# Mixed k/q tail tile first, in the single banks; z and kv of the first two head pairs ahead of later projections

## The chip, the cores and the metric

The kernel runs on one core of one Trainium2 chip. The metric is device time in microseconds (us) of one execution. Times of a kernel are the median of several runs; the profile is of one further execution. The engines are PE (TensorE, matmul), DVE (VectorE), ACT (ScalarE), POOL (GpSimd) and SP (SyncE, which here issues most DMAs).

## What is computed

A feature-map attention, and on its output a two-layer feed-forward network with a leaky activation. Batch 8, 8 heads, 576 tokens, head width 64, 128 features:

```python
def phi(x):
    proj = np.einsum('bhsd,df->bhsf', x, w_phi)
    proj = proj - np.max(np.abs(proj), axis=-1, keepdims=True)
    return np.concatenate([np.exp(proj), np.exp(-proj)], axis=-1)
q_p, k_p = (phi(q), phi(k))
kv = np.einsum('bhsf,bhsd->bhfd', k_p, v)
z = np.sum(k_p, axis=2)
num = np.einsum('bhsf,bhfd->bhsd', q_p, kv)
den = np.einsum('bhsf,bhf->bhs', q_p, z)[..., None] + 1e-06
x = num / den                      # then reshaped to 4608 tokens x 512
h = x @ w_in
g = np.maximum(h, 0.0) + alpha * np.minimum(h, 0.0)
out = g @ w_out                    # w_in 512 x 2048, w_out 2048 x 512
```

All is float32. The feed-forward matmuls split every operand into a high and a low part and add three products.

## The kernel before

Attention works on 32 **pairs** of heads; the two heads of a pair are h = 0 and 1. A pair's k and q are loaded as one tile `raw` of 1152 columns: 512 of k, then 64 of k's tail and 64 of q's tail, then 512 of q. `project` multiplies them by `w_phi` in nine tiles of 128 columns per head: chunk 0 is k's first four tiles; chunk 1 is the **mixed tile** (both tails) and q's four tiles. A projection lies in PSUM until DVE has taken the maximum of its absolute values (L324) and written the difference to an SBUF tile `t` (L325). Then ACT takes the exponentials: `xk` from chunk 0 (L338) and `k` from the mixed tile (L333). PE sums k's features (`k_z`, L378: z) and multiplies them with v (`k_acc`, L361: kv). ACT copies the result (`ks`), PE transposes it (`kt`), ACT copies that (`sf`). PE also transposes the q part of `t` (`qt`: `q_turn(2)` is the mixed tile, `q_turn(0)` and `q_turn(1)` the four q tiles of each head), ACT takes its exponentials (`qf`), and PE forms the denominator (`d`, L444) and the numerator (`n`, L426).

Where the projections lie in PSUM: a pair of banks for one chunk of both heads, tile `pj` (pool `ps_pj`, one buffer, so the next chunk waits until DVE has read it); chunk 0 of the first two pairs lies in the two single banks of `psf` instead. Chunk 1 has ten tiles, two more than fit, and the fifth of each head lies in a single bank of `ps_m`, tile `pl`. `ps_m` has three buffers that `pl`, `kt`, the mixed `qt`, `d` and `n` take in turn. Before, `pl` holds the last q tile (j = 4), and the mixed tile (j = 0) lies in `pj` with three q tiles. `ps_kv` has one buffer for z and kv.

The two PE passes that a float32 matmul takes here are counted apart in the trace (x16 for eight matmuls).

What sets the order: every step of every pair is a function with a due time, i + an entry of `places(i)`; decoding of the 64-bit weights (`aw`, `ew`: L177 on ACT, L185 to L188 on DVE, L193 on POOL, L128 the cast, L132 the low part) and the feed-forward steps have due times as well. All are sorted, and the instructions of PE, SP, DVE and ACT stand in that order; each engine works through its list in order:

```python
with tc.manual_schedule(engines=pinned):
    for _, u in sorted(todo, key=lambda tu: tu[0]):
        u()
```

For the first nine pairs (`i < ZP`) z is summed by PE over all five k tiles. The feed-forward network's first part runs among the later pairs, its second part after them.

Of the kernel before, what the change touches and what calls it, by code (L numbers as in the profile page):

```python
# [38 lines left out]
WA = (0.0040, 0.50)  # L39
# [19 lines left out]
def places(i):  # L59
    early = i < ZP  # L60
    end = i >= NPAIR - 2
    return dict(
        ld=-1.90,
        lv=-0.80,
        p=(-0.9955 if early else -0.993, 0.0),
        ke=(-0.26, 0.0011),
        ks=(0.0015, 0.0022, 0.0026),
        kz=1.0002,
        ka=1.0012,
        ko=1.0025,  # L70
        kr=1.10,
        kc=1.16,
        q=(1.34, 1.50, 1.20),
        qe=(1.46, 1.62, 1.28),
        d=2.0004,
        ds=2.0008,
        n=2.005,
        s=2.0055,
        d9=2.25,
        dv=3.0016 if early else 3.20 if end else 2.80,  # L80
        rd=3.0017 if early else 3.21 if end else 2.82,
        rr=3.20 if early else 3.45 if end else 3.001,
        x=3.45 if early else 3.60 if end else 3.20,
        xs=3.90 if early else 3.85 if end else 3.45,
    )


F0 = 9.23
# [25 lines left out]
def fused_kernel(ctx: ExitStack, tc: tile.TileContext, kq, v, w_phi, w_in, w_out, alpha, out):  # L114
# [110 lines left out]
    def decode_at(t, blk):  # L225
        return [(t + (WT if t < TL else WL)[k], lambda u=u: u(*blk, WN)) for k, u in stages.items()]
# [58 lines left out]
    def attention_units(i):  # L285
# [12 lines left out]
        def project(ch):  # L298
            t = c["t", ch] = wk.tile([P, 2, 4 + ch, FD], F32, tag=f"t{ch}", name=f"t{i}_{ch}", bufs=1 + ch)
            dst, out, js = {}, [], [0, 1, 2, 3]  # L300
            if ch:
                js = [4] + js
                for h in range(2):
                    p1 = ps_m.tile([P, 1, 1, FD], F32, tag="m", name=f"pl{i}_{h}")
                    dst[h, 4] = p1[:, 0, 0]
                    out.append((slice(h, h + 1), slice(4, 5), p1))
            if ch == 0 and i < 2:
                for h in range(2):
                    p1 = psf.tile([P, 1, 4, FD], F32, tag="f", name=f"pj{i}_{ch}_{h}")
                    dst.update({(h, j): p1[:, 0, j] for j in range(4)})  # L310
                    out.append((slice(h, h + 1), slice(0, 4), p1))
            else:
                p2 = ps_pj.tile([P, 2, 4, FD], F32, tag="pj", name=f"pj{i}_{ch}")
                dst.update({(h, j): p2[:, h, j] for h in range(2) for j in range(4)})
                out.append((slice(0, 2), slice(0, 4), p2))
            for j in js:
                for h in range(2):
                    hs = slice(h * D, (h + 1) * D)
                    ts = slice((4 * ch + j) * P, (4 * ch + j + 1) * P)
                    pe.matmul(dst[h, j], lhsT=c["raw"][hs, ts], rhs=w_sb[hs], start=True, stop=True)  # L320
            for n, (hs, js, src) in enumerate(out):
                nh, nj = hs.stop - hs.start, js.stop - js.start
                m = wk.tile([P, nh, nj], F32, tag="m", name=f"m{i}_{ch}_{n}", bufs=4)
                dve.tensor_reduce(m, src, axis=AX.X, op=ALU.max, apply_absolute_value=True)  # L324
                dve.tensor_tensor(  # L325
                    t[:, hs, js], src, m.unsqueeze(3).broadcast_to([P, nh, nj, FD]), op=ALU.subtract
                )
# [150 lines left out]
        def store():  # L478
            nc.sync.dma_start(x_d[hp, :, b * S : (b + 1) * S], c["s"])

        at = places(i)
        us = [
            (at["ld"], load),
# [17 lines left out]
        for n in range(2):  # L501
            us.append((at["p"][n], lambda n=n: project(n)))
# [128 lines left out]
    todo = []  # L631
# [6 lines left out]
    first = [(ff, z, o) for z in range(2) for ff in range(NF1) for o in range(0, 512, WN)]  # L638
# [1 line left out]
    late += [(ff, z) for z in (1, 0) for ff in range(NF1 + NA, NF - NL)]  # L640
    blocks = [(ff, z, o) for ff, z in late for o in range(0, 512, WN)]
    for n, blk in enumerate(first):
        todo += decode_at(1 + n // 2 + WA[n % 2], blk)
    for n, blk in enumerate(blocks):
        todo += decode_at(W2A + W2D * n, blk)
    todo += first_x()
# [188 lines left out]
```

## Time and profile before

| | us |
|---|---|
| median of 3 runs | 1132.63 |
| lowest, highest of them | 1130.05, 1133.77 |
| the profiled execution | 1131.19 |
| its span in the profile | 1129.4 |
| PE busy in that span | 1115.0 |
| DVE, ACT, POOL busy | 643.2, 560.4, 211.0 |

The profiled execution's own time is 1.8 us above its span. The mean granted clock of PE is 0.997 of full speed over the span. Busy times overlap, since the engines work side by side; where PE is busy nearly all the time, what counts is when it is idle or at a lower clock, and what it waited for.

### The profile page before, as it was taken

The numbers are of one execution on the slowest core, as the hardware profiler recorded it, in microseconds if no ns is written. First come the engines' busy times: TensorE is split into PE (matmuls) and PEld (weight loads), VectorE is DVE, ScalarE is ACT, GpSimd is POOL, SyncE is SP. The second block draws the span as 40 slices with busy tenths as digits, with TensorE's granted clock in tenths as the row PEclk, the third lists the DMA queues.
The fourth block names the chain that finished last, engine by engine and source line by source line (L and its number), as shares of the span: only waits on it lengthen the run. The fifth ranks groups of instructions, "written<-read, shape, count | busy, mean of one in ns | idle before, by whom it ended". The sixth has DMA issues, their size and how long they took to land.

```text
span 1129.4 us, 18395 instructions
## 1 busy us (share of the span) xinstructions
PE 1115.0 (99%) x7246; PEld 868.8 (77%) x7246; DVE 643.2 (57%) x983; ACT 560.4 (50%) x1148; POOL 211.0 (19%) x217
## 2 busy tenths in 40 slices
PE   8999999999999999999999999999999999999998
PEld 6766777777777777677778888888888888888886
DVE  7888958798788787836862332424233423343323
ACT  4777665666666665665543342333333333333331
POOL 1244332322324242243541000000000000000000
PEclk8999999999999999999999999999999999999999
DMA  5566265546546365467627030303030302020011
GB/s 191 146 184 208 86 202 154 172 151 192 176 148 199 109 204 164 147 212 218 223 66 256 27 109 1 112 1 112 1 112 1 112 1 97 16 91 21 11 64 38
DMA packets 74389, 133.68 MB, mean 118 GB/s; under 512 B 14656, under 2 KB 25024, under 8 KB 73664
## 3 DMA queue, kind: packets, MB, share of 16 engines
q1 hardware_dynamic: 72000, 122.48, 33.9%
q0 software_dynamic: 2016, 9.96, 2.6%
q8 instruction: 57, 0.93, 0.3%
q14 instruction: 28, 0.23, 0.1%
q10 hardware_dynamic: 288, 0.07, 0.0%
HBM read 93.92 MB, written 38.42 MB: 117 GB/s over the span
## 4 chain that ended last, share of the span: by engine, by line
PE 93%; DVE 4%; ACT 1%; DMA 1%; issue 1%; POOL 0%; DVEq 0%; ACTq 0%
PE h L516 12%; PE h L518 11%; PE h L517 11%; PE po L523 8%; PE po L525 8%; PE po L527 8%; PE kv L361 6%; PE pj L320 5%; PE n L426 5%; PE o L523 4%; PE o L527 3%; PE o L525 3%; PE d L444 2%; PE qt L407 2%; PE kv L378 2%; PE pl L320 1%
## 5 line engine op out<-in xcount | busy, mean ns | idle before, releaser
L247 DVE SCALAR_TENSOR_TENSOR g<-r,aln,g 128x512 f32<-128x512 f32 x144 | 112.2, 779 | 309.2 <-ACT g L243 308.9
L242 ACT ACTIVATE r<-h 128x512 f32<-128x512 f32 x143 | 86.0, 601 | 279.1 <-PE h L518 279.0
L132 DVE TENSOR_TENSOR gl<-g,gh 128x512 fp32r<-128x512 f32 x144 | 105.1, 730 | 81.3 <-ACT gh L128 80.8
L128 ACT CAST gh<-g 128x512 fp32r<-128x512 f32 x144 | 90.0, 625 | 94.4 <-DVE g L247 94.4
L243 ACT ACTIVATE g<-h 128x512 f32<-128x512 f32 x144 | 86.0, 597 | 7.1 <-DVE r L240 6.4
L523 PE MATMUL po<-gh,wd 128*128 128x512 f32 x216 | 84.3, 390 | 0.2 <-ACT gh L128 0.2
L525 PE MATMUL po<-gh,wd 128*128 128x512 f32 x216 | 84.3, 390 | 0.0
L527 PE MATMUL po<-gl,wd 128*128 128x512 f32 x216 | 83.9, 390 | 0.0
L324 DVE TENSOR_REDUCE m<-pj 128x8 f32<-128x1024 f32 (+1 forms) x66 | 78.1, 1184 | 9.2 <-PE pj L320 9.1
L193 POOL TENSOR_TENSOR aw<-ew,aw 128x256 f32<-128x256 f32 x64 | 55.9, 874 | 131.8 <-DVE ew L188 130.3
L325 DVE TENSOR_TENSOR t<-pj,m 128x1024 f32<-128x1024 f32 (+1 forms) x66 | 78.7, 1192 | 2.3
L320 PEld LDWEIGHTS pj<-w_sb,raw 64*128 64x128 f32 x1024 | 63.4, 190 | 18.6 <-issue 13.8
L320 PE MATMUL pj<-w_sb,raw 64*128 64x128 f32 x1024 | 72.8, 281 | 4.7 <-DVE t L325 4.5
L523 PE MATMUL o<-gh,w 128*128 128x512 f32 x180 | 76.0, 422 | 0.2
L516 PE MATMUL h<-xh,w 128*128 128x512 f32 x180 | 75.8, 421 | 0.0
L527 PE MATMUL o<-gl,w 128*128 128x512 f32 x180 | 71.2, 396 | 3.1 <-DVE gl L132 2.9
L476 POOL TENSOR_TENSOR s<-s,rr 128x576 f32<-128x576 f32 x32 | 47.6, 1486 | 142.0 <-DMA rr<-rec_d 131.4
L417 ACT ACTIVATE qf<-qt 128x512 f32<-128x512 f32 x128 | 68.5, 615 | 6.3 <-PE qt L407 6.3
L518 PE MATMUL h<-xl,w 128*128 128x512 f32 x180 | 70.7, 393 | 0.0
L525 PE MATMUL o<-gh,w 128*128 128x512 f32 x180 | 70.6, 392 | 0.0
L517 PE MATMUL h<-xh,w 128*128 128x512 f32 x180 | 70.5, 392 | 0.0
L523 PE MATMUL po<-gh,w 128*128 128x512 f32 x180 | 70.1, 389 | 0.0
(110 smaller groups left out, 2415.5 us busy)
## 6 DMA issues: line engine op xcount, KB each, us to landing
xr<-x_d SPq DMA_DIRECT2D x18, 1024.0 KB
raw<-kq_dram SPq DMA_DIRECT2D x31, 576.0 KB
v<-v_dram SPq DMA_DIRECT2D x32, 320.0 KB
w_d<-raww SPq DMA_DIRECT2D x38, 256.0 KB
rr<-rec_d SPq DMA_DIRECT2D x64, 144.0 KB
x_d<-s SPq DMA_DIRECT2D x32, 288.0 KB
part_d<-os SPq DMA_DIRECT2D x36, 256.0 KB
pt<-part_d SPq DMA_DIRECT2D x9, 1024.0 KB
```

The source lines that it names most:

```text
L128: return act.copy(dst, src)
L132: return eng.tensor_tensor(dst, src, f(hi), op=ALU.subtract)
L242: act.activation(st["r"], ps, AF.Relu, scale=-1.0)
L243: act.activation(st["g"], ps, AF.Relu)
L247: dve.scalar_tensor_tensor(g, st["r"], aln[:, ff : ff + 1], g, op0=ALU.mult, op1=ALU.add)
L320: pe.matmul(dst[h, j], lhsT=c["raw"][hs, ts], rhs=w_sb[hs], start=True, stop=True)
L516: pe.matmul(ps, lhsT=wt[0][:, ws], rhs=xh, start=n == 0, stop=False)
L517: pe.matmul(ps, lhsT=wt[1][:, ws], rhs=xh, start=False, stop=False)
L518: pe.matmul(ps, lhsT=wt[0][:, ws], rhs=xl, start=False, stop=n == NK - 1)
L523: pe.matmul(ps, lhsT=wt[2][:, ws], rhs=gh, start=first, stop=False)
L525: pe.matmul(ps, lhsT=wt[3][:, ws], rhs=gh, start=False, stop=False)
L527: pe.matmul(ps, lhsT=wt[2][:, ws], rhs=gl, start=False, stop=last)
```

## The change

It has three parts. In chunk 1 the mixed tile goes to the single banks `pl` and is multiplied first, and q's four tiles go to the pair of banks `pj`. For pairs 0 and 1 other due times are put in place of those of `places`: z, kv and the copy of the first pair come before the projection of pair 1's chunk 1 (0.737), pair 1's z before chunk 0 of pair 2 and its kv right behind it, and the steps of pair 0 behind them move (`kr` to `n`). The decode of the first weight block is due 0.024 earlier.

```diff
@@ places
     early = i < ZP
     end = i >= NPAIR - 2
+    first = {}
+    if i == 0:
+        first = dict(
+            kz=0.7370, ka=0.7372, ko=0.7374, kr=1.0030, kc=1.0034,
+            n=2.0041, q=(1.0032, 1.0033, 1.0031), qe=(1.0036, 1.0037, 1.0035),
+        )
+    if i == 1:
+        first = dict(kz=0.0044, ka=0.0046, ko=0.0048)
     return dict(
...
-    )
+    ) | first
@@ project
             if ch:
-                js = [4] + js
+                js = js + [4]
                 for h in range(2):
                     p1 = ps_m.tile([P, 1, 1, FD], F32, tag="m", name=f"pl{i}_{h}")
-                    dst[h, 4] = p1[:, 0, 0]
-                    out.append((slice(h, h + 1), slice(4, 5), p1))
+                    dst[h, 0] = p1[:, 0, 0]
+                    out.append((slice(h, h + 1), slice(0, 1), p1))
...
                 p2 = ps_pj.tile([P, 2, 4, FD], F32, tag="pj", name=f"pj{i}_{ch}")
-                dst.update({(h, j): p2[:, h, j] for h in range(2) for j in range(4)})
-                out.append((slice(0, 2), slice(0, 4), p2))
+                dst.update({(h, ch + j): p2[:, h, j] for h in range(2) for j in range(4)})
+                out.append((slice(0, 2), slice(ch, ch + 4), p2))
@@ the list of steps
     for n, blk in enumerate(first):
-        todo += decode_at(1 + n // 2 + WA[n % 2], blk)
+        todo += decode_at(1 + n // 2 + (WA[n % 2] if n else -0.02), blk)
```

The instructions stay the same in number and shape, and the orders of SP and POOL do not change. PE's, DVE's and ACT's lists differ only up to the first transposes of pair 1 (`kt` of pair 1). Three places follow. In the names, `pj_0`, `pl_0` and so on carry the chunk or head, and the last number is the tile's; line numbers are 8 higher in the changed kernel.

PE, from the end of pair 1's chunk 0 (`raw_157` is pair 1's, `raw_206` pair 2's; `kv_242` and `kv_214` are pair 0's z and kv), before:

```order
L320 MATMUL pj_0_1_191<-w_sb,raw_157 128x128
L320 MATMUL pl_0_220<-w_sb,raw_157 128x128
L320 MATMUL pl_1_221<-w_sb,raw_157 128x128
L320 MATMUL pj_1_222<-w_sb,raw_157 128x128 x8
L378 MATMUL kv_242<-xk_161,ones 32x128 x16
L378 MATMUL kv_242<-k_0_130,ones 32x128 x4
L361 MATMUL kv_242<-xk_161,v_159 64x256 x8
L361 MATMUL kv_242<-k_0_130,v_159 64x256 x2
L320 MATMUL pj_0_283<-w_sb,raw_206 128x128 x8
L393 MATMUL kt_295<-ident,ks_275 128x128 x3
```

The same place of the changed kernel:

```order
L328 MATMUL pj_0_1_191<-w_sb,raw_157 128x128
L386 MATMUL kv_214<-xk_161,ones 32x128 x16
L386 MATMUL kv_214<-k_0_130,ones 32x128 x4
L369 MATMUL kv_214<-xk_161,v_159 64x256 x8
L369 MATMUL kv_214<-k_0_130,v_159 64x256 x2
L328 MATMUL pl_0_258<-w_sb,raw_157 128x128
L328 MATMUL pl_1_259<-w_sb,raw_157 128x128
L328 MATMUL pj_1_260<-w_sb,raw_157 128x128 x8
L401 MATMUL kt_282<-ident,ks_245 128x128 x3
L412 MATMUL qt_2_286<-ident,t_1_164 128x128 x2
```

Pair 0's z and kv now stand ahead of pair 1's chunk 1, and pair 2's chunk 0 has gone from between kv and `kt`.

DVE, from the last subtraction of pair 1's chunk 0 (`aw_0_0`, `ew_0_0` are the first weight block), before:

```order
L325 TENSOR_TENSOR t_0_189<-pj_0_1_191,m_0_1_203 128x512
L324 TENSOR_REDUCE m_1_0_233<-pl_0_220 128x1
L325 TENSOR_TENSOR t_1_219<-pl_0_220,m_1_0_233 128x128
L324 TENSOR_REDUCE m_1_1_236<-pl_1_221 128x1
L325 TENSOR_TENSOR t_1_219<-pl_1_221,m_1_1_236 128x128
L324 TENSOR_REDUCE m_1_2_239<-pj_1_222 128x8
L325 TENSOR_TENSOR t_1_219<-pj_1_222,m_1_2_239 128x2x512
L185 TENSOR_SCALAR aw_0_0_215<-aw_0_0_215 128x256
L186 SCALAR_TENSOR_TENSOR aw_0_0_215<-raww_0_0_210,aw_0_0_215 128x256
L187 TENSOR_SCALAR ew_0_0_277<-aw_0_0_215 128x256
L188 SCALAR_TENSOR_TENSOR ew_0_0_277<-raww_0_0_210,ew_0_0_277 128x256
L324 TENSOR_REDUCE m_0_0_292<-pj_0_283 128x8
```

The same place of the changed kernel:

```order
L333 TENSOR_TENSOR t_0_189<-pj_0_1_191,m_0_1_203 128x512
L193 TENSOR_SCALAR aw_0_0_212<-aw_0_0_212 128x256
L194 SCALAR_TENSOR_TENSOR aw_0_0_212<-raww_0_0_210,aw_0_0_212 128x256
L195 TENSOR_SCALAR ew_0_0_252<-aw_0_0_212 128x256
L196 SCALAR_TENSOR_TENSOR ew_0_0_252<-raww_0_0_210,ew_0_0_252 128x256
L332 TENSOR_REDUCE m_1_0_271<-pl_0_258 128x1
L333 TENSOR_TENSOR t_1_257<-pl_0_258,m_1_0_271 128x128
L332 TENSOR_REDUCE m_1_1_274<-pl_1_259 128x1
L333 TENSOR_TENSOR t_1_257<-pl_1_259,m_1_1_274 128x128
L332 TENSOR_REDUCE m_1_2_277<-pj_1_260 128x8
L333 TENSOR_TENSOR t_1_257<-pj_1_260,m_1_2_277 128x2x512
L332 TENSOR_REDUCE m_0_0_339<-pj_0_330 128x8
```

The four decode instructions have moved from behind pair 1's chunk 1 to ahead of it, so that pair 1's chunk 1 and pair 2's chunk 0 stand next to each other.

PE, from pair 1's z to the numerator of pair 0, in the changed kernel (`kv_308` is pair 1's, `raw_354` pair 3's; before, the order was z of pair 1, `d`, kv of pair 1, chunk 0 of pair 3, `n`, with pair 2's chunk 1 ahead of all):

```order
L386 MATMUL kv_308<-xk_247,ones 32x128 x16
L386 MATMUL kv_308<-k_1_132,ones 32x128 x4
L328 MATMUL pj_0_330<-w_sb,raw_206 128x128 x8
L369 MATMUL kv_308<-xk_247,v_208 64x256 x8
L369 MATMUL kv_308<-k_1_132,v_208 64x256 x2
L328 MATMUL pl_0_381<-w_sb,raw_206 128x128
L328 MATMUL pl_1_382<-w_sb,raw_206 128x128
L328 MATMUL pj_1_383<-w_sb,raw_206 128x128 x8
L452 MATMUL d_403<-qf_301,sf_299 32x288 x8
L434 MATMUL n_0_421<-qf_301,sf_299 64x288 x4
L434 MATMUL n_1_426<-qf_301,sf_299 64x288 x4
L328 MATMUL pj_0_432<-w_sb,raw_354 128x128 x8
```

Pair 2's chunk 1 now stands behind pair 1's kv, and the numerator of pair 0 stands ahead of pair 3's chunk 0.

## Rows read from the trace of the kernel before

**Rows 1.** The page, part 1: busy time, share, instructions by engine.

```profile
PE 1115.0 (99%) x7246; PEld 868.8 (77%) x7246; DVE 643.2 (57%) x983; ACT 560.4 (50%) x1148; POOL 211.0 (19%) x217
```

**Rows 2.** Timeline of PE: start, us, instructions, [idle before <- releaser].

```profile
8.25 1.01 PE L320 MATMUL pj<-w_sb,raw 64*128 64x128 f32 x13 [0.36 <-DVE t L325]
...
11.69 2.08 PE L320 MATMUL pj<-w_sb,raw 64*128 64x128 f32 x16 [2.09 <-DVE t L325]
...
22.81 1.16 PE L320 MATMUL pj<-w_sb,raw 64*128 64x128 f32 x16 [0.59 <-DVE t L325]
...
29.50 2.16 PE L426 MATMUL n<-qf,sf 128*64 128x288 f32 x16
31.60 0.55 PE L393 MATMUL kt<-ident,ks 128*128 128x128 f32 x3
...
33.49 1.06 PE L320 MATMUL pj<-w_sb,raw 64*128 64x128 f32 x16
...
98.93 1.16 PE L320 MATMUL pj<-w_sb,raw 64*128 64x128 f32 x16 [1.05 <-DVE t L325]
...
394.95 1.16 PE L320 MATMUL pj<-w_sb,raw 64*128 64x128 f32 x16 [0.37 <-DVE t L325]
...
467.27 0.50 PE L527 MATMUL o<-gl,w 128*128 128x512 f32 x1 [1.56 <-DVE gl L132]
```

**Rows 3.** Windows: length, busy time (x) PE PEld DVE ACT POOL, PEclk, DMA, GB/s.

```profile
10.50:11.00 0.50, 0.00 (x0) 0.00 (x0) 0.50 (x1) 0.00 (x0) 0.00 (x0) 0.76 0.92 354
...
13.50:14.00 0.50, 0.50 (x12) 0.28 (x12) 0.47 (x2) 0.00 (x0) 0.00 (x0) 0.50 0.05 20
...
17.50:18.00 0.50, 0.50 (x8) 0.32 (x6) 0.47 (x3) 0.27 (x1) 0.00 (x0) 0.92 0.72 230
...
466.00:467.00 1.00, 0.00 (x0) 0.00 (x0) 1.00 (x2) 0.00 (x0) 0.00 (x0) 1.00 0.48 49
```

**Rows 4.** Chain that ended last, 0 to 40 us: start, us, what.

```profile
13.77 2.29 PE kv L378 x40
16.06 3.07 PE kv L361 x20
...
23.97 1.23 PE kv L378 x40
...
26.17 2.31 PE kv L361 x20
```

**Rows 5.** Timeline of DVE, 8 to 34 us.

```profile
10.32 1.22 DVE L325 TENSOR_TENSOR t<-pj,m 128x1024 f32<-128x1024 f32 x1
...
13.58 0.69 DVE L325 TENSOR_TENSOR t<-pj,m 128x512 f32<-128x512 f32 x1
14.18 0.28 DVE L324 TENSOR_REDUCE m<-pl 128x1 f32<-128x128 f32 x1
...
15.23 1.21 DVE L324 TENSOR_REDUCE m<-pj 128x8 f32<-128x1024 f32 x1
...
17.62 0.28 DVE L185 TENSOR_SCALAR aw<-aw 128x256 uint32<-128x256 uint32 x1
...
18.72 0.43 DVE L188 SCALAR_TENSOR_TENSOR ew<-raww,ew 128x256 f32<-128x256 uint32 x1
20.28 1.22 DVE L324 TENSOR_REDUCE m<-pj 128x8 f32<-128x1024 f32 x1 [1.13 <-PE pj L320]
21.54 1.22 DVE L325 TENSOR_TENSOR t<-pj,m 128x1024 f32<-128x1024 f32 x1
...
30.88 1.22 DVE L325 TENSOR_TENSOR t<-pj,m 128x1024 f32<-128x1024 f32 x1
```

**Rows 6.** Timeline of ACT, 7 to 20 us.

```profile
8.14 2.00 ACT L338 ACTIVATE xk<-t 128x1024 f32<-128x1024 f32 x2 [5.19 <-DVE t L325]
11.58 0.72 ACT L333 ACTIVATE k<-t 64x256 f32<-64x256 f32 x2 [1.44 <-DVE t L325]
...
19.19 0.48 ACT L388 COPY ks<-kv 128x384 f32<-128x384 f32 x1 [0.73 <-PE kv L361]
```

**Rows 7.** Waits, 100 to 450 us: us in total, times, longest us.

```profile
ACT k L333 <- DVE t L325: 39.0, 21, 3.8
```

## The prediction

> **What bounds the kernel now.** I read the page's busy times first. PE is busy for 1115.0 of 1129.4 us [rows 1], so a change can save only what PE idles (14.4 us in all) or loses at a lower clock. The second view is PE's timeline with the idle time ahead of each entry [rows 2]. Of the longer idle stretches two lie where the change moves work: 2.09 us ahead of pair 1's chunk 1 at 11.69, and 0.59 us ahead of pair 2's chunk 1 at 22.81. Both end with DVE's subtraction, because the pair of banks has one buffer. Between 22.81 and 95 us PE does not wait at all. The later waits are 1.05 us at 98.93, 0.37 at 394.95 and 1.56 at 467.27, the last in feed-forward work.
>
> The third view is the granted clock. It falls during the 2.09 us: the window from 10.5 to 11.0 has a mean of 0.76, so with levels 1 and 0.5 the fall lies at 10.76; the window from 17.5 to 18.0 has 0.92, so the return lies at 17.58 [rows 3]. For 6.8 us PE ran at 1.2 instead of 2.4 GHz. What that cost is read from like work in both states: the projection took 2.08 us against 1.16 [rows 2], z 2.29 against 1.23, kv 3.07 against 2.31 [rows 4]. Together 0.92 + 1.06 + 0.76 = 2.74 us.
>
> So PE lost 2.09 + 0.59 + 2.74 = 5.4 us here, 0.48% of the time. That is the whole prize of the start. The fourth view, DVE's timeline, says how much of it is out of reach [rows 5]: from 10.32 to 32.10 (30.88 + 1.22, the end of pair 3's chunk 0) DVE has hardly any idle time but 1.13 us. DVE is nearly as much the limit of these 22 us as PE.
>
> **The change, part by part.** *Mixed tile in the single banks.* Number and shape of matmuls and DVE operations stay. DVE takes the single banks first, so the mixed tile's `t` is there one pair-of-banks operation earlier, and ACT's `k` need not wait for it. In pair 0 ACT ends `xk` at 8.14 + 2.00 = 10.14, waits 1.44 us and ends `k` at 12.30 [rows 6]; now `k` ends at 10.14 + 0.72 = 10.86. In the later pairs ACT's waits for `t`, 39.0 us over 21 waits [rows 7], mostly go. ACT is not what PE waits for there: the only wait for attention inside that stretch that rows 2 show is 0.37 us, on DVE. I cost the steady part at 0, with bounds of 0 and a gain of 0.37 + 1.05. The four q tiles now all come from the pair of banks, which was the last to be read before too, so the transposes of q are no later.
>
> *z and kv of pair 0 ahead.* PE ends pair 1's chunk 0 at about 9.3 (8.25 + 1.01 [rows 2]) and then waits for `xk` until 10.2: 0.9 us idle in place of 2.09. At full clock z ends at 10.2 + 1.23 = 11.4 (`k` is there at 10.86) and kv at 11.4 + 2.31 = 13.7 [rows 4]. Pair 1's chunk 1 then finds its banks free, since DVE has left them at 11.54 (10.32 + 1.22): `pl` takes 0.3 (4 of 16 parts of a 1.16), `pj` 1.16, to 15.2. `kt` follows to 15.7.
>
> *The decode ahead of pair 1's chunk 1 on DVE.* DVE ends pair 1's chunk 0 at 13.58 + 0.69 = 14.27 and now runs the four decode instructions, 18.72 + 0.43 - 17.62 = 1.53 us [rows 5], to 15.8. Their data must have landed: the queue moves 20 GB/s from 13.5 to 14.0 [rows 3], so the burst is over by then. Queued behind them on DVE is `pl` of pair 1, 15.23 - 14.18 = 1.05 us for both heads. The mixed `qt` of pair 0 waits for the buffer of the first `pl`, free at 15.8 + 0.52 = 16.3: **PE idles 0.6 us**. The transposes end at about 17.5 and z of pair 1 at 18.7. (`kt` and transposes take 33.49 - 31.60 - 0.3 = 1.6 us [rows 2].)
>
> *Pair 2's chunk 0 behind pair 1's z.* DVE ends pair 1's chunk 1 at 16.85 + 2.48 = 19.3 (2.48 is 21.54 + 1.22 - 20.28 [rows 5]). The banks free then: **PE idles 0.65**, projects from 19.35 to 20.5, and **DVE idles 1.2** meanwhile, since the decode that used to stand in this place is gone from it. Before, the like idle was 1.13 in spite of the decode, because of PE's half clock; so the gain of the clock is lost to the order here. DVE ends pair 2's chunk 0 at 23.0. PE does kv of pair 1 (to 22.8), `pl` (23.1), `pj` of pair 2 (24.2) and `d` (25.2; its length is 26.17 - 23.97 - 1.23 = 0.97 [rows 4]).
>
> *The second decode block.* Its scale on ACT stands behind `ks` of pair 1, which waits for kv at 22.8; `ks` takes 0.48 [rows 6], the scale about as much, so DVE **idles 0.75** to 23.75, decodes to 25.3, and takes 0.15 for `aln`. The first half of n needs the buffer of pair 2's first `pl`, free at 25.45 + 0.52 = 26.0: **PE idles 0.8**. n takes 31.60 - 29.50 = 2.1 [rows 2], to 28.1. DVE ends `pl` at 26.5 and pair 2's chunk 1 at 29.0, so pair 3's chunk 0 starts at 29.0: **PE idles 0.9**. It ends at 30.15; `kt`, transposes and `pl` bring PE to 32.05. DVE decodes to 30.5 and ends pair 3's chunk 0 at 33.0: **PE idles 1.0** and starts pair 3's chunk 1 at 33.05.
>
> *Sum.* The same step started at 33.49 before [rows 2]. From here both lists are the same and PE is the limit, so the gain is 33.49 - 33.05 = **0.45 us**: 1131.19 - 0.45 = 1130.7 for a run like the profiled one. That run lies 1.44 below the median shown, so in terms of the median I say 1132.63 - 0.45 = **1132.2 us**. Of the 5.4 us lost before, 0.9 + 0.6 + 0.65 + 0.8 + 0.9 + 1.0 = 4.85 come back as idle stretches of PE.
>
> *The clock.* The sum holds the clock at full speed. In the trace the 2.09 us stretch went with a fall, and the 1.56 us one at 467.27 did not: in the window from 466 to 467 PE is idle throughout and the clock stays at 1.00 [rows 2, 3]. Each new stretch is 1.0 or shorter, so by the rows I expect no fall, though there are six within 23 us. The Trainium skill, TensorE: Matmul & The Clock Gate, section "A second HAM failure mode: psum-queue depth-cycling", says that short idles between groups of matmuls, as PSUM banks are cycled, can make the clock swing between its levels. By the rows the sum stays a gain of 0.45; by that rule the rivals with falls below come in. No run here shows yet which holds for gaps of this length.
>
> **The rivals.**
>
> *One fall of the clock, as before.* If the first idle stretch still tips the clock at 10.76, and it returns at 17.58, then z, kv and pair 1's projection pay up to 2.74 us. DVE's decode hides part: `pj` of pair 1 would end at 17.9 instead of 15.2, where DVE comes to it at 16.85, so some 1.1 is lost there and more at the small steps behind: 1.1 to 2.7, say 1.9. Time 1132.2 + 1.9 = 1134.1, slower by 0.13%, which a measurement of this kernel can hardly tell from no change (0.3%, 3.4 us).
>
> *Faster: DVE gives way.* If the changed order kept DVE busy, without any of the 1.13 us idle, it would end pair 3's chunk 0 at 30.97, and PE could start the next step at 31.0: a gain of 2.5. With the later DVE waits gone too (1.05 + 0.37, since ACT runs ahead) it is 3.9: 1128.7 us. Against it: the two DVE idle stretches above follow from one buffer for the pair of banks, and the change adds none.
>
> *Slower: a swinging clock.* The six stretches lie close together between 9 and 33 us. One mechanism turns the sign: PE at 1.2 GHz for a second spell like that of before. Each spell costs up to 2.74 us in 6.8 us. The first, partly hidden, costs 1.9; a second, at 25 to 32 us, falls on d, n and projections with PE waited for by DVE, and costs 2.74: 1132.2 + 1.9 + 2.74 = 1136.8 us. It is slower by over 0.3% from 3.4 + 0.45 = 3.85 us of unhidden loss on, about nine and a half us at half clock.
>
> **How the numbers follow.** The forecast (no fall, gain 0.45) has 0.58; one fall 0.22; the faster case 0.10; the swinging clock 0.10. The first two are within 0.3%, hence faster 0.10, same 0.80, slower 0.10. The predicted time is 1132.2. The range has to take in the spread of the runs of before, 1130.05 to 1133.77, the bound of the waits (a gain of 2.5 alone gives 1130.1, with the later ones 1128.7) and one fall with its whole price (1132.2 + 2.7 = 1134.9): 1128.8 to 1135.2, which leaves out the far end of the faster case and the swinging clock.
>
> **What the profile after would show.** Right: z of pair 0 starts near 10.2; the 2.09 us stretch is gone; PE has idle stretches of 0.5 to 1 us ahead of the mixed `qt` of pair 0, pair 2's chunk 0, n of pair 0, pair 3's chunk 0 and pair 3's chunk 1, all ended by DVE; DVE idles about 1.2 us ahead of pair 2's chunk 0 and 0.75 ahead of the second decode; pair 3's chunk 1 starts near 33; ACT's waits of `k` for `t` shrink from 39 us to a few, with PE's time unmoved by that. Wrong: a window of half clock between 10 and 35 us (a rival with falls); pair 3's chunk 1 starting before 32 (DVE was not the limit); PE's idle stretches past 90 us gone or grown by over 1 us (ACT's lead counts after all); or PE busy time itself changed by over 3 us, which no step here provides for.

## The result, and the profile after

The changed kernel takes 1133.74 us as median of 20 runs (1131.75 to 1136.20), the kernel before 1131.28 beside it (20 runs, 1129.56 to 1133.77): a ratio of 1.0020, 95% interval 1.0013 to 1.0027. It is slower by about 2.3 us, where 0.45 us of gain were forecast. That is within the range and within 0.3%, but on the other side, and the interval excludes no change. (A ratio compares all executions of two kernels; it need not be the quotient of the two medians.)

The page of the changed kernel, its span and part 1 (compare [rows 1]):

```profile
span 1134.3 us, 18397 instructions
...
PE 1117.1 (98%) x7246; PEld 868.7 (77%) x7246; DVE 639.2 (56%) x983; ACT 561.9 (50%) x1148; POOL 213.0 (19%) x217
```

This profiled execution took 1136.04 us, near the top of its runs. PE is busy 2.1 us longer than before and idle 17.2 instead of 14.4 us. The timeline of PE (start, us, instructions, idle before it and what ended that), answering to [rows 2]:

```profile
8.97 1.13 PE L328 MATMUL pj<-w_sb,raw 64*128 64x128 f32 x14 [0.91 <-DVE t L333]
...
10.91 0.96 PE L386 MATMUL kv<-xk,ones 128*32 128x128 f32 x27 [0.47 <-ACT xk L346]
...
17.09 0.41 PE L412 MATMUL qt<-ident,t 128*128 128x128 f32 x2 [0.79 <-DVE t L333]
...
19.96 1.16 PE L328 MATMUL pj<-w_sb,raw 64*128 64x128 f32 x16 [0.35 <-issue]
...
27.08 2.16 PE L434 MATMUL n<-qf,sf 128*64 128x288 f32 x16 [0.96 <-DVE t L333]
...
29.94 1.16 PE L328 MATMUL pj<-w_sb,raw 64*128 64x128 f32 x16 [0.70 <-PE n L434]
...
33.80 1.16 PE L328 MATMUL pj<-w_sb,raw 64*128 64x128 f32 x16 [0.71 <-DVE t L333]
...
469.06 0.51 PE L535 MATMUL o<-gl,w 128*128 128x512 f32 x1 [1.90 <-DVE gl L140]
```

The 2.09 us stretch is gone, and the small stretches are where the prediction put them: ahead of the mixed `qt`, pair 2's chunk 0, `n` and both chunks of pair 3. The stretch in feed-forward work, 1.56 us before, is now 1.90. The trace puts two of the waits down to "issue" and to `n`; both end 0.1 us behind the DVE subtraction that frees the banks (18.63 + 1.22 and 28.62 + 1.22). The windows show the clock (columns as in [rows 3]; PEclk is third from the end):

```profile
0.00:40.00 40.00, 33.77 (x422) 25.59 (x424) 30.62 (x59) 22.75 (x47) 7.86 (x17) 1.00 0.45 149
469.00:470.00 1.00, 0.94 (x6) 0.87 (x7) 0.66 (x2) 0.30 (x1) 0.00 (x0) 0.86 0.77 170
470.00:471.00 1.00, 1.00 (x4) 0.81 (x4) 0.65 (x1) 1.00 (x4) 0.30 (x1) 0.50 1.03 397
```

No fall at the start; but one behind the 1.90 us stretch, to 1.2 GHz until 473.1. The execution before had none there: its clock stays at 1.00 from 17.58 to 1130.3. On DVE (answering to [rows 5]) the decode stands ahead of pair 1's last tiles, and the two forecast idle times are there, 1.30 and 0.67 us:

```profile
14.89 0.28 DVE L193 TENSOR_SCALAR aw<-aw 128x256 uint32<-128x256 uint32 x1
...
21.16 1.23 DVE L332 TENSOR_REDUCE m<-pj 128x8 f32<-128x1024 f32 x1 [1.30 <-PE pj L328]
...
24.38 0.29 DVE L193 TENSOR_SCALAR aw<-aw 128x256 uint32<-128x256 uint32 x1 [0.67 <-ACT aw L185]
```

ACT's waits for `t` from 100 to 450 us fell from 39.0 us [rows 7] to (waits: us in total, times, longest)

```profile
ACT k L341 <- DVE t L333: 5.5, 8, 1.5
```

Pair 3's chunk 1 starts at 33.80 against 33.49 before, but DVE's first reduction of a projection came later, here before and, below, after:

```profile
5.37 0.69 DVE L324 TENSOR_REDUCE m<-pj 128x4 f32<-128x512 f32 x1 [4.36 <-PE pj L320]
```
```profile
6.08 0.69 DVE L332 TENSOR_REDUCE m<-pj 128x4 f32<-128x512 f32 x1 [5.07 <-PE pj L328]
```

The **distance** between the two, which leaves out how late the first load lands, went from 28.12 to 27.72 us. This distance is the yardstick for the start in all that follows.

### The profile page after: what moved, and what is told of

The parts are those of the page before. It is cut to its first block, busy times and chain, and to the rows that moved or that the text cites. A ratio compares the mean times of both kernels' runs of the same rounds, so it can differ in the third digit from the quotient of the medians.

```text
span 1134.3 us, 18397 instructions
## 1 busy us (share of the span) xinstructions
PE 1117.1 (98%) x7246; PEld 868.7 (77%) x7246; DVE 639.2 (56%) x983; ACT 561.9 (50%) x1148; POOL 213.0 (19%) x217
## 4 chain that ended last, share of the span: by engine, by line
PE 89%; DVE 7%; ACT 2%; DMA 1%; issue 1%; DVEq 0%; SPq 0%; ACTq 0%
PE h L524 11%; PE h L526 11%; PE h L525 11%; PE po L531 8%; PE po L535 8%; PE po L533 8%; PE kv L369 6%; PE pj L328 5%; PE n L434 5%; PE o L531 3%; PE o L535 3%; PE o L533 3%; PE d L452 2%; PE qt L415 2%; DVE m L332 2%; PE kv L386 1%
```

## The experiments

**One part at a time.** The tile swap alone on the kernel before (`js + [4]`, the mixed tile in `pl`, all orders of before):

> The kernel before with the mixed tile in the single banks alone; all engine orders as before. Theory A (the start's new order is what costs, the tile costs nothing): 0 within 1 us of before; ACT's waits of k for t shrink from 39 us in 100 to 450 us to below 5, PE's idle time from 34 to 1000 us stays at that of before, 4.5 us, within 0.5. Theory B (the tile costs in the 32 pairs, because ACT runs ahead and moves POOL's and DVE's work into each other): slower by 1.5 to 3 us, with most of it between 60 and 570 us. Theory C (the clock: the loss at the start moves to the 1.6 to 1.9 us idle stretch near 467 us): 0 within 1 us, since the start is that of before.

1132.74 us against 1131.76, ratio 1.0005 (0.9994 to 1.0016). Distance 26.89: shorter by 1.2 than in the first profile of before, with no change of order. Its stretch near 467 us is 1.93 us. Theory B's size fails by the trace: from `kt` of pair 2 to `kt` of pair 29 (42 to 463 us) it takes 0.07 us less than the second profile of before (shown below), and e13, of the same order, 0.37 less. A and C are not told apart here.

The new order with the old tile (`js = [4] + js`, the mixed tile in `pj`):

> The changed kernel with the mixed tile back in the pair of banks; all engine orders as in the changed kernel. Theory A: slower than before by 2 to 3.5 us, as much as the whole change or up to 1 us more, since k of pair 0 comes 1.4 us later, z of pair 0 waits for it and the first idle stretch of PE grows to about 2 us in two pieces. Theory B: within 1 us of before. Theory C: slower by 1 to 3 us, by one fall of the clock near 467 us in most runs.

1134.00, ratio 1.0017 (1.0007 to 1.0028). The order alone slows the kernel about as much as the whole change; that the swap alone costs something too, e1's interval leaves open. Theory C fails: a fall shows as a mean granted clock of 0.998 or less (worked out below), and one execution of 12 has that. The distance is 28.79, 1.1 longer than in the changed kernel: the swap does help the new order at the start, as `k` comes earlier, yet the medians agree (next run), so it seems to cost about as much elsewhere.

The changed kernel with the first decode block at its old due time, and the changed kernel once more:

```diff
-        todo += decode_at(1 + n // 2 + (WA[n % 2] if n else -0.02), blk)
+        todo += decode_at(1 + n // 2 + WA[n % 2], blk)
```

> The changed kernel with the first decode block due at its old time, so that its four DVE instructions stand again between pair 1's chunk 1 and pair 2's chunk 0. By the prediction's step (DVE idles 1.2 us ahead of pair 2's chunk 0 because the decode is gone from there, and PE idles 0.6 us ahead of the mixed transposes because it stands ahead of pl): both go, DVE's idle falls to below 0.3 us, pair 3's chunk 1 starts 1.0 to 1.4 us sooner than in the changed kernel (33.80 in its profile, with a start 0.7 late). Theory A: 1 to 1.4 us faster than the changed kernel, still slower than before by about 1. Theory B: less than 0.5 us of it is left at the end.

> The changed kernel itself once more, for a second profile. All theories: slower than before by 2.5 us, 1.5 to 3.5. Theory C: the clock falls near 467 us again, to a mean of 0.5 for 3 us, at a cost of 1.6 us. Theory A: PE's stall pattern up to 34 us is the same to 0.1 us, and the offset to before at the transposes of pair 8 (about 108 us) is 0.5 us or more once the different start of the load is taken off. Theory B: the offset grows by over 1 us between 108 and 460 us.

1131.13, ratio 0.9995 (0.9984 to 1.0006), and 1134.03, ratio 1.0012 (1.0002 to 1.0022). Distances 26.37 and 27.73. The place of four DVE instructions costs 1.36 us at the start; with the decode back, PE's waits ahead of the mixed `qt` and pair 2's chunk 0 and DVE's 1.30 us are gone. In the second profile of the changed kernel the clock did not fall near 468 us, though the stretch there is 1.96 us: theory C is not a matter of every execution.

**What the clock at the start costs.** A second profile of the kernel before, unchanged:

> The kernel before, unchanged, for a second profile of it. Theory A (the half-clock spell of 6.8 us from 10.76 to 17.58 in the first profile is longer than usual): the spell at the start is about 3.4 us, as in the kernel with the tile swap alone, the mean granted clock 0.998, and pair 3's chunk 1 starts about 1 us earlier against the first projection than before (27.4 instead of 28.1 us after DVE's first reduction of a projection, less or more 0.4). Theory B (6.8 us is what this stall brings): the spell is again 6 to 7 us and the distance stays.

PE's rows of pair 1's and pair 3's chunk 1, the windows at the start, and DVE's first reduction and the one of pair 2's chunk 0:

```profile
12.78 1.16 PE L320 MATMUL pj<-w_sb,raw 64*128 64x128 f32 x16 [2.08 <-DVE t L325]
...
33.46 1.06 PE L320 MATMUL pj<-w_sb,raw 64*128 64x128 f32 x16
```
```profile
13.00:14.00 1.00, 1.00 (x20) 0.88 (x22) 0.89 (x3) 0.39 (x2) 0.00 (x0) 1.00 0.91 332
14.00:15.00 1.00, 1.00 (x28) 1.00 (x28) 0.96 (x3) 0.00 (x0) 0.00 (x0) 0.56 0.28 56
15.00:16.00 1.00, 1.00 (x22) 0.62 (x14) 0.96 (x4) 0.61 (x1) 0.00 (x0) 0.50 0.83 207
...
17.00:18.00 1.00, 1.00 (x10) 0.64 (x8) 0.97 (x2) 0.71 (x2) 0.00 (x0) 0.73 0.98 258
```
```profile
6.46 0.69 DVE L324 TENSOR_REDUCE m<-pj 128x4 f32<-128x512 f32 x1 [5.45 <-PE pj L320]
...
20.24 1.22 DVE L324 TENSOR_REDUCE m<-pj 128x8 f32<-128x1024 f32 x1
```

Half clock from 14.12 to 17.54, 3.4 us, where the first profile had 6.8 [rows 3]; the idle stretch ahead of it is the same 2.08 us. The distance is 27.00 (33.46 - 6.46), 1.12 less. Theory A held. DVE's wait of 1.13 us ahead of pair 2's chunk 0 [rows 5] is not there: it is what the long spell added.

The kernel before with its idle stretch filled by matmuls that nothing reads:

```diff
+    def keep_busy():
+        for n in range(7):
+            pe.matmul(ps_w[:, 1], lhsT=warm, rhs=warm, start=True, stop=True)
+
+    todo.append((0.5, keep_busy))
```

> The kernel before with seven additional warm-up matmuls into the warm-up tile behind pair 1's chunk 0, which fill its 2.09 us idle stretch with work that nothing reads. The order of all else is that of before. Theory A (the clock's fall costs about 1.2 us in most executions): the clock stays at 1.00 up to 40 us, PE waits about 0.5 to 1 us more for DVE at pair 2's projections, and the kernel is 0.3 to 1.2 us faster than before (0.03 to 0.1%). Theory B (the fall costs 2.74 us, as the prediction had it): 2 to 2.7 us faster (0.2%). Theory C (the clock's price is hidden by DVE altogether): within 0.3 us of before.

1132.58, ratio 1.0004 (0.9995 to 1.0013). That excludes theory B; of A only the low end is left, and C fits. The window from 8 to 40 us, PE's row of pair 2's chunk 0 and DVE's row ahead of it:

```profile
8.00:40.00 32.00, 29.54 (x400) 21.94 (x402) 29.44 (x56) 21.60 (x46) 6.54 (x9) 1.00 0.44 139
```
```profile
17.87 1.16 PE L320 MATMUL pj<-w_sb,raw 64*128 64x128 f32 x16 [1.41 <-issue]
```
```profile
16.55 1.22 DVE L325 TENSOR_TENSOR t<-pj,m 128x1024 f32<-128x1024 f32 x1
```

With the clock at 1.00 throughout, PE now stands 1.41 us ahead of pair 2's chunk 0, until DVE's last read of these banks, which ends at 17.77 (16.55 + 1.22); and the distance is 26.89, that of a 3.4 us spell. DVE, busy for 29.44 of these 32 us, hides the short spell wholly.

The decode's early place on the kernel before:

> The kernel before with the first decode block due 0.024 earlier, which puts its four DVE instructions ahead of pair 1's last tiles; PE's order is that of before. Theory A (the place of the decode costs PE time by itself, 1.4 us in the changed order): DVE idles ahead of pair 2's chunk 0 or soon behind it, PE waits some 0.5 to 1.4 us longer up to pair 3's chunk 1, and the kernel is 0.3 to 1.4 us slower than before (0.03 to 0.12%). Theory B (the decode costs only together with the new order of z and kv): within 0.3 us of before.

1132.95, ratio 1.0012 (1.0002 to 1.0021). The ratio speaks for theory A; its profile had the long spell (6.8 us) and a distance of 28.36, only 0.24 longer than the first profile's. So the decode ahead seems to slow this order too, but where is not shown.

All distances, with the half-clock spell at the start of each profile:

| kernel | half clock, us | distance, us |
|---|---|---|
| before, first profile | 6.8 | 28.12 |
| before, second profile | 3.4 | 27.00 |
| tile swap alone (e1; e13 below) | 3.4; 3.4 | 26.89; 26.90 |
| before with a later move (e10 below) | 3.4 | 26.90 |
| before, decode ahead (e6) | 6.8 | 28.36 |
| before, stretch filled (e7) | 0 | 26.89 |
| changed (first, e0; e9 and e12 below) | 0 | 27.72, 27.73; 27.76, 27.76 |
| order alone (e2) | 0 | 28.79 |
| changed, decode back (e3) | 0 | 26.37 |
| e3 with second decode earlier (e5; e8, e11 below) | 0 | 25.70; 25.72, 25.72 |

**A better start.** e3 with `decode_at(1 + n // 2 + (0.006 if n == 1 else WA[n % 2]), blk)`, so that ACT's scale of the second block stands ahead of pair 1's `k`:

> The changed kernel with the first decode block at its old place and the second decode block's scale on ACT ahead of the exponential of pair 1's mixed tile, so that DVE's second decode needs not wait for it. PE's and DVE's orders are those of the run with the decode back. Theory A (that wait of DVE is what delays n of pair 0 and pair 3's projections): DVE's idle time of 0.7 us ahead of the second decode goes, PE's three waits of 0.98, 0.70 and 0.71 lose 0.5 to 0.7 us in sum, and the median is about 0.6 us below that of the run with the decode back, 0.7 to 1.5 us (0.06 to 0.13%) below the kernel before. Theory B (PE's waits there come from the one buffer of the pair of banks): the waits stay and so does the median.

The distance fell by 0.67 as theory A said, with PE's 0.98 us ahead of `n` down to 0.19; the waits of 0.70 and 0.71 behind it stay (0.71 and 0.79). But the time is 1132.02, ratio 1.0000 (0.9990 to 1.0009). A start 1.3 us shorter than the usual one of before gained nothing that the interval shows; so something later seems to eat it.

**The stretch near 468 us.** In the five profiles so far with the swapped tile (first, e0, e1, e3, e5) it is 1.89 to 1.96 us, in before (two profiles) and e6 1.53 to 1.56, in e7 and e2, with the old tile too, 1.65 and 1.73. Behind it the clock fell in the first profile and in e3, whose windows are

```profile
467.00:468.00 1.00, 1.00 (x7) 0.89 (x8) 0.43 (x1) 0.53 (x2) 0.00 (x0) 0.94 1.02 391
468.00:469.00 1.00, 1.00 (x4) 0.70 (x4) 0.85 (x2) 1.00 (x4) 0.53 (x1) 0.50 1.03 397
...
471.00:472.00 1.00, 1.00 (x5) 0.76 (x5) 0.00 (x0) 1.00 (x2) 0.69 (x1) 0.85 0.09 4
```

From `kt` of pair 29 to `kt` of pair 30 these two took 1.90 and 1.97 us longer than the first profile of before; e0, e1 and e5, without a fall, 0.40, 0.36 and 0.33 longer. The fall costs some 1.55 us and the longer stretch 0.35.

The mean granted clock of an execution tells whether the clock fell in it. Behind PE's last matmul it falls too, for up to 2.4 us in the profiles, which costs nothing and takes up to 0.001 off the mean. So, where the start has no spell, 0.999 or more is read as no fall, and 0.998 or less as a fall somewhere. Four runs test what the stretch does. The transposes `qt` of pair 29 are moved ahead of the waiting step,

```diff
-        q=(1.34, 1.50, 1.20),
+        q=(1.25, 1.251, 1.20) if i == 29 else (1.34, 1.50, 1.20),
```

in the changed kernel (e9), in e5 (e8) and in before (e10), beside e5 once more (e11):

> The changed kernel with both q transposes of pair 29 (1.04 us of PE work) moved ahead of the feed-forward step whose last matmul waits 1.90 us for DVE near 468 us; nothing else moves. Theory A (the idle stretch there, 1.90 us instead of 1.56, lets the clock fall in about half of the executions, which costs 1.5 to 2.5 us when it falls): the stretch is 0.9 us, the mean granted clock is 1.000 in nearly all executions, none is above 1134.5, and the median is about 1 us below the changed kernel's, 1132.7 to 1133.2 against 1131.5 of before. Theory B (the late loss comes from transfers, and the clock near 468 us matters little): the stretch shrinks, the median stays at 1133.7 to 1134.

> The run with the first decode block back and the second block's scale earlier, and with the q transposes of pair 29 ahead as well. Theory A: its executions without a clock fall had 1129.6 to 1131.9 us and the others 1131.3 to 1134.0; without falls the median is 1130 us, 1.5 us (0.13%) below the kernel before. Theory B: same as without the move, 1132.

> The kernel before with the same move of pair 29's q transposes. Its stretch near 467 us is 1.56 us and was not followed by a clock fall in either profile. Theory A (the move gives back only the clock): within 0.5 us of before. Theory B (the move itself makes PE's work near 467 us shorter): as much faster as the other two runs of this call against theirs.

> The run with the second block's scale earlier, once more, for the comparison with its variant that moves the q transposes, on the same chip: again 1132 us as median, with executions in two groups by the mean granted clock, about 1129.7 at 1.000 and 1132 or more at 0.998 and 0.999.

Before stood at 1131.75 (35 runs). e9: 1131.21, ratio 1.0000 (0.9989 to 1.0011); e8: 1129.82, 0.9984 (0.9974 to 0.9994); e10: 1130.72, 0.9989 (0.9978 to 0.9999); e11: 1131.51, 0.9996 (0.9985 to 1.0006). PE's row in e9:

```profile
467.77 0.49 PE L535 MATMUL o<-gl,w 128*128 128x512 f32 x1 [1.08 <-DVE gl L140]
```

In e9 and e8 every execution has a mean granted clock of 0.999 or 1.000, where 14 of 32 of the changed kernel have 0.998 or less. So the falls went, and most of them were near 468 us. Not all: in the profile of e11 the clock fell at 89.89, behind another stretch, and not behind its 1.91 us near 468; nor do its executions form the two groups that were expected (1129.44 to 1132.07 at 1.000, 1130.97 to 1132.88 at 0.998). e9's median lies below the range of theory A, and one execution, 1135.05, above its bound. But before gained 1 us too, with its clock as before (0.996 to 0.998): theory A was wrong there, the filled stretch (1.56 to 0.67 us) is a gain of its own, 0.92 us from `kt` to `kt` of pairs 29 and 30. In the changed kernel it is 1.90 to 1.08, 0.8 us, and the ratio moved by 0.0020, 2.3 us (by 0.0012, 1.4 us, against its second measurement): the rest would be the clock, but the intervals leave room from none to 3 us.

**Why the stretch grew.** DVE's sum `z` of pair 28 and the POOL subtraction near it, in the changed kernel and, below, with the order alone:

```profile
447.35 1.03 DVE L359 TENSOR_TENSOR z<-y 128x512 f32<-128x512 f32 x1
```
```profile
446.85 0.98 POOL L140 TENSOR_TENSOR raww<-aw,raww 128x256 fp32r<-128x256 f32 x1 [2.50 <-ACT raww L136]
```
```profile
447.41 0.69 DVE L359 TENSOR_TENSOR z<-y 128x512 f32<-128x512 f32 x1
```
```profile
448.26 1.23 POOL L140 TENSOR_TENSOR raww<-aw,raww 128x256 fp32r<-128x256 f32 x1 [3.85 <-ACT raww L136]
```

All eight profiles with the swapped tile up to here have 1.03 or 1.04, all six without it 0.69. `k` no longer waits for pair 28's last `t`, so ACT comes earlier to the cast that releases POOL, and POOL's subtraction now lies beside `z`. The Trainium skill, GPSIMD Engine Reference, section "1. Specifications", has it that GpSimd and VectorE share their SBUF interfaces, with contention where the VectorE instruction has two SBUF inputs or runs in a 2-port mode; the trace agrees for `z`, which has two, 1.03 against 0.69 us. From here to the stretch DVE has one idle time, 0.69 us, and that ends with ACT's cast of DVE's own result, so a delay of DVE is carried on. Two runs move that cast behind the next two feed-forward activations on ACT, in the changed kernel and in the tile swap alone:

```diff
+        us = decode_at(W2A + W2D * n, blk)
+        if n == 23:
+            us = [(t + (0.12 if 4 <= k <= 5 else 0.0), u) for k, (t, u) in enumerate(us)]
+        todo += us
-        todo += decode_at(W2A + W2D * n, blk)
```

> The changed kernel with one ACT cast (and the POOL subtraction that follows it) of the weight block near 447 us moved three places down ACT's list, behind the two feed-forward activations; PE's, DVE's and SP's orders stay. Theory A (the swap of the tiles lets ACT run ahead, POOL's subtraction then falls beside DVE's sum z, which takes 1.03 instead of 0.69 us, and DVE brings this 0.34 us to the stretch near 468 us): z is 0.69 again, the stretch 1.55 to 1.6 instead of 1.90, the mean granted clock is 1.000 in more of the executions, and the median is 0.4 to 1.3 us below the changed kernel's, 1132.4 to 1133.5. Where POOL's subtraction lengthens the DVE operations behind z by as much, z is 0.69 and the stretch is still 1.9. Theory B (PE just comes to the stretch earlier): the stretch stays 1.9 and the median about 1133.8.

> The kernel before with the tile swap alone and the same move of the ACT cast near 447 us. Theory A: z is 0.69 instead of 1.03 us, the stretch near 467 us 1.55 to 1.6 instead of 1.93, executions with a mean granted clock of 0.996 or less (5 of 12 with the tile swap alone) become rare, and the median is 0.4 to 1.2 us below that of the tile swap alone, 1131.5 to 1132.3, like before or slightly below. Theory B: the stretch stays 1.9 and so does the median.

1133.11, ratio 1.0011 (1.0002 to 1.0020), and 1132.87, ratio 1.0002 (0.9989 to 1.0015): neither tells from its parent. Executions at 0.996 or less, 5 of 12 in e1, are 2 of 11 in e13 (beside them in before: 5 of 35 and 1 of 21), too few to tell. DVE in e12:

```profile
446.08 0.69 DVE L359 TENSOR_TENSOR z<-y 128x512 f32<-128x512 f32 x1
...
449.89 0.54 DVE L193 TENSOR_SCALAR aw<-aw 128x256 uint32<-128x256 uint32 x1
```

`z` is 0.69 again, but POOL's subtraction now lies beside `aw`, 0.54 instead of 0.28, and the stretch is 1.87 (e13: 1.82): the proviso in the expectation. The sizes fit: against the second profile of before, `aw` carries 0.26 and the passage from `kt` of pair 29 to `kt` of pair 30 is 0.29 longer in e13, `z` carries 0.34 and it is 0.38 longer in e1. But the stretch also grew to 1.65 and 1.73 in e7 and e2, with `z` at 0.69, and that a place without contention would bring 1.56 back was not shown.

## Why the prediction was wrong

**The order at the start: right.** Against the profiled execution the distance shrank by 0.40 us where the prediction had 0.45. The stretches came as forecast in place and order (0.47, 0.79, 0.35, 0.96, 0.70, 0.71 for 0.9, 0.6, 0.65, 0.8, 0.9, 1.0), and so did DVE's two idle times (1.30 and 0.67 for 1.2 and 0.75). With the first reduction 0.71 us later than before, pair 3's chunk 1 starts at 33.09 by the prediction's count, which had 33.05.

**The sum's base: wrong, and this turned the sign of the start.** "The same step started at 33.49 before ... so the gain is 33.49 - 33.05" took one execution with 6.8 us of half clock for the kernel. Five other profiles with before's order at the start (second of before, e1, e7, e10, e13) have 3.4 us or none, and distances of 26.89 to 27.00. Against these the changed order, 27.72, loses 0.7 us. Which spell is the usual one the mean granted clocks tell: of 120 runs of before beside the experiments, 83 have 0.998 or more, as the second profile, and 6.8 us at half clock alone would take them to 0.997. The other 37, at 0.997 or less, can have the long spell, or a short one and a further loss. The base in terms of the median was off as well: 1132.63 came from three runs, where 20 gave 1131.28. That 1132.2 missed the measured 1133.74 by 1.5 us, and not by the 2.9 that separate 1131.28 - 0.45 from it, is luck.

**The price of the clock, 2.74 us: wrong.** It was summed over PE's instructions as though PE were the limit. By the distances the short spell costs 0.1 us at most (27.00 against 26.89 in e7) and the long one 1.1 to 1.2. The prediction itself read that DVE is nearly as much the limit there, and used it for the gaps but not for the clock: DVE's 1.13 us of idle time, which it set against the 1.2 us of the new order, belongs to the long spell alone. "The whole prize of the start" of 5.4 us was never there: filling the 2.09 us and keeping the clock up gains nothing in e7.

**The decode ahead on DVE: rightly traced, its part not seen.** Its 1.53 us of work is followed correctly to the wait for the first `pl`, and DVE's idle time is rightly put down to its new place; but the prediction never asked what the order would do without it. It costs 1.36 us of the distance, so the other parts alone would have gained 0.6 against the usual 27.00 (e3).

**The steady part of the tile swap, costed at 0 with bounds on the side of a gain: wrong.** ACT's waits went as said, and from 100 to 450 us PE waits no longer for attention than before (0.4 us). What was not asked is what ACT's lead sets off: a POOL subtraction beside DVE's `z`, 0.34 us that DVE carries to the 1.56 us stretch. So the term that was put at 0 measured 0.35 us of loss, and more where the clock falls. The prediction quoted that stretch as evidence that such a length does not tip the clock, but did not ask whether the change moves it. It became 1.90, and behind 1.90 the clock falls in some executions. Of 32 executions of the changed kernel, nine with a mean clock of 1.000 have a median of 1133.07 and fourteen with 0.998 or less 1134.85.

**The sum as it stands.** 0.7 at the start (0.4 if all 37 of those runs of before had the long spell) and 0.35 at the stretch; a fall of 1.55 in 14 of 32 executions adds up to 0.7. Together that is 1.4 to 1.8 us, where the first measurement has 2.3 (1.5 to 3.1) and the second, e0, 1.4 (0.2 to 2.5). So no further cause is needed, though one of some 0.5 us is not excluded. The same three terms, each from the run's own distance (against 27.00), passage from `kt` to `kt` without a fall (against the second profile of before) and share of falls, can be added up for the other runs with the new order:

| run | sum, us | measured (95% interval), us |
|---|---|---|
| order alone (e2) | 2.1 | 1.9 (0.8 to 3.2) |
| decode back (e3) | 0.3 | -0.6 (-1.8 to 0.7) |
| second decode earlier (e5) | -0.2 | 0.0 (-1.1 to 1.0) |
| the same (e11) | -0.3 | -0.5 (-1.7 to 0.7) |
| with the transposes ahead (e8) | -1.8 | -1.8 (-2.9 to -0.7) |
| changed, transposes ahead (e9) | 0.3 | 0.0 (-1.2 to 1.2) |
| changed, cast later (e12) | 1.7 | 1.2 (0.2 to 2.3) |

Every sum lies within its interval. One loss besides moves from execution to execution whatever the kernel. ACT's wait near 87 us for a load of x is 0.89 and 1.95 us in the two profiles of the changed kernel, 0.47 and 0.39 in those of before, but 2.01 in e7 and 2.58 in e11, while e9, with the same start, has 0.37. From `kt` of pair 6 to `kt` of pair 8, around this wait, the changed kernel took 0.35 and 1.10 us longer than the second profile of before, e7 1.37, e11 3.05, and e9 0.28: single profiles differ here by more than the change costs.

**The rivals with a falling clock.** Six stretches of 0.35 to 0.96 us within 25 us left the clock at 1.00 up to 40 us, so neither came at the start. The Trainium skill, TensorE: Matmul & The Clock Gate, section "A second HAM failure mode: psum-queue depth-cycling", tells of a kernel whose clock swung as PE idled briefly and often between groups of matmuls; the trace does not show that for gaps of this length. The rival of one fall gave 1134.1 us, near the result, but with the fall at 10.76: the one that came lies 459 us later, behind a single stretch twice as long, so the nearness is luck. The faster rival wanted DVE to lose its 1.13 us of idle time; by their mean clocks most executions of before never had it, and the changed order gave DVE 1.30 and 0.67.

**A version that beats both.** e8 (new order and tile, decode back, second scale earlier, pair 29's transposes ahead) takes 1129.82 us, ratio 0.9984 (0.9974 to 0.9994) to before. The move of the transposes alone (e10) gives a good part of that; the two are not told apart by their intervals.

## What to carry to other kernels

Before crediting a recovered clock or stall, take a second profile of the same kernel and measure from an event inside it, such as the first reduction: here two profiles of one kernel differ by 1.1 us over 27, more than the change was worth. A half-clock spell costs only what the other engine does not hide (here 0.1 us at most of 3.4 us, 1.1 to 1.2 of 6.8). When an engine that nobody waits for is given a lead, follow what it releases, down to the idle stretches behind which the clock has so far stayed up.

## What the hardware showed that was not expected

The same 2.08 us stretch at the same place was followed by half clock for 3.4 us in four profiles and for 6.8 in two. The two long spells began 1.16 us (10.76, first profile of before) and 1.22 us (10.89, e6) into the stretch, the four short ones later: 1.75 to 1.80 us into it (e1, e10, e13) or 1.3 us after PE was busy again (14.12, second profile of before). Near 468 us, stretches of 1.90 and 1.92 us were followed by a fall and ones of 1.87, 1.89, 1.91, 1.93 and 1.96 were not, with the same list of PE there: in this range the length of the stretch alone does not decide. Near 88 us a stretch of 1.60 us, behind ACT's wait for x, was followed by a fall in e11, while 1.65 and 1.73 near 468 us were not (e7, e2):

```profile
88.21 0.68 PE L452 MATMUL d<-qf,sf 128*32 128x288 f32 x4 [1.60 <-ACT qf L425]
```
```profile
89.00:90.00 1.00, 0.81 (x12) 0.30 (x12) 0.11 (x1) 1.00 (x3) 0.19 (x1) 0.94 0.25 83
90.00:91.00 1.00, 1.00 (x6) 0.30 (x4) 0.00 (x0) 1.00 (x2) 1.00 (x1) 0.50 0.07 27
```

A DVE instruction of 0.69 us with two inputs in SBUF (`z`) takes 1.03 beside a POOL subtraction, and one of 0.28 us with one input (`aw`) 0.54.
